# Blockwise attention, then hash-routed experts, on one core: transposes a pair earlier, and another order of weight loads

## The chip, the core and the metric

The kernel runs on one core of a Trainium2 chip. A core has a matrix engine (TensorE), three engines for elementwise work (VectorE, ScalarE, GpSimd), an engine that mainly issues transfers (SyncE), and 16 DMA engines that all of them share. Each engine takes its own instructions in order; they wait for each other by semaphores. On-chip memory is SBUF (operands) and PSUM (where TensorE writes its results).

The metric is the device time of one execution in microseconds (us). Before the change it is 337.07 us, the median of three runs (336.7 to 337.87).

## What is computed

Attention over 8 batches of 8 heads, 576 positions, head width 64, masked by blocks of 64; then every one of the 4608 rows of width 512 goes through one of 8 experts, chosen by a hash of its token id.

```python
scores = scale * np.matmul(q, k.transpose(0, 1, 3, 2))
mask = block_i >= block_j
attn = np.exp(scores - max)           # masked, then divided by the row's sum
x = (attn @ v) as rows [B * S, H * D]
expert_idx = token_ids * 2654435761 % 8
for e in range(8):
    xe = x[expert_idx == e]
    out[expert_idx == e] = np.maximum(xe @ w1[e], 0.0) @ w2[e]
```

## The kernel before

The order of all instructions is written out by hand; each engine runs its own share of that one list.

**Attention.** The work is cut into 32 pairs of heads, `g` from 0 to 31, four pairs to a batch; the loop at L505 has one turn for each and one more to drain. In turn `g` TensorE makes the scores of pair `g` in three chunks (`S_chunk`, L191), ScalarE takes the exponential of each chunk (L200), and TensorE multiplies the exponentials of pair `g - 1` by the values (`PV`, L227). The values carry a column of ones, so that the row sums come out of the same matmul. VectorE divides (`norm`, L247: a reciprocal at L254, a product at L255). `S_rest` (L202) makes the last diagonal block of all four pairs of a batch at once.

The scores need q and k with the head width on the partitions. `T_group(b, n)` (L150) makes a quarter of that for batch `b`: 18 transposes on TensorE (L159), then one copy out of PSUM on VectorE (L164; for batch 0 half of it on ScalarE). Groups 2 and 3 are k, 0 and 1 are q. The four groups of batch `b` stand at the ends of turns `4b - 4` to `4b - 1`, that is, up to the last turn before the batch begins. There is one PSUM buffer (`tp`) for them and one (`O`) for the outputs; score chunks have two.

**Loads.** `load_qk` and `load_v` fetch a batch on GpSimd's queue and turn it into bf16 on the way: two transfers of 576 KB for k and q, six for v. Each transfer from that queue takes the next of eight semaphores in turn, and waits until the transfer that had it before has landed. A finished batch of rows is written to a DRAM buffer by `write_x` (L260), the first five batches from SyncE, the last three from GpSimd.

**Routing.** `route()` (a generator, advanced step by step in the first turns) works out the place of each token in a table of 640 places per expert. Then for each batch `j` `place_a` (VectorE, turn `5 + 2j`), `place_p` (GpSimd, turn `6 + 2j`) and `place_b` (turn `9 + 2j`) add the rows to the table `perm3`. `place_b` is five matmuls (L412) into spare columns of the `O` buffer, and a sum into `acc` on VectorE (L415). It stands ahead of `PV`.

**Experts.** For each expert, rows are fetched by `perm3` (`gather_x`, L461, five indirect transfers of 128 rows), transposed (`transpose_x`, L553 and L554), multiplied by the first weights and passed through the relu (`stage_a`, L566 and L571; for experts 0 and 1 in two parts, L585 and L589), multiplied by the second weights (`stage_b`, L599), copied out of PSUM (L604) and scattered to the output (L606, five indirect transfers). The loop runs `stage_a(e)`, `transpose_x(e + 1)`, `stage_b(e - 1)`. There are two buffers for first weights and two for second ones, so `load_w1(e + 2)` waits for `stage_a(e)` to end, and the gathers for expert `e + 2` stand behind it on GpSimd, and the scatters of expert `e - 1` behind those.

The SBUF of the attention's buffers is used again for the experts' ones, so the first copy at L554 waits until the last rows are out of it.

Of the kernel before, what the change touches and what calls it, by code (L numbers as in the profile page):

```python
# [10 lines left out]
F32 = mybir.dt.float32  # L11
# [23 lines left out]
WARM = 40  # L35
# [5 lines left out]
def kernel(  # L41
# [30 lines left out]
    ov_i = const.tile([1, OVT + 1], I32, name="ov_i")  # L72
    inc = const.tile([P, E], F32, name="inc")

    nc.gpsimd.iota(jmp[:], pattern=[[1, P]], base=0, channel_multiplier=-1,
                   allow_small_or_imprecise_dtypes=True)
    nc.vector.tensor_single_scalar(identbf[:], jmp[:], 0.0, op=ALU.is_equal)
    nc.vector.tensor_single_scalar(lower[:], jmp[:], 0.0, op=ALU.is_gt)
    nc.vector.memset(onesbf[:], 1.0)

    nc.vector.memset(maskk[:], 0.0)
    nc.vector.memset(maskq[:], 0.0)
# [144 lines left out]
    def PV(g, m):  # L227
        b, pr = divmod(g, NP)
        h = pr + NP * m
        pt = pts[g % 2]  # L230
        vx, v4 = vexts[b % NV]
        if g not in ots:
            ots[g] = psO.tile([P, 2, 512], F32, name="O", tag="O")
        O = ots[g][:, m, 0 : 5 * (D + 1)].rearrange("p (t d) -> p t d", t=5)
        for t in range(5):
            for n, (o0, i) in enumerate(PVS[t]):
                nc.tensor.matmul(  # L237
                    O[:, t, :], lhsT=pt[:, m * PTW + o0 : m * PTW + o0 + 128], rhs=vx[:, h, i, 0 : D + 1],
                    start=(n == 0), stop=(n == t),
                )  # L240
            if t == 4:
                nc.tensor.matmul(
                    O[:, t, :], lhsT=pt4s[b % 2][:, pr * 64 : pr * 64 + 128],
                    rhs=v4[:, pr, m, 0 : D + 1], start=False, stop=True,
                )

    def norm(g):  # L247
        b, pr = divmod(g, NP)
        if b not in xss:
            xss[b] = xfix[b % 3]  # L250
        xs = xss[b]
        O = ots.pop(g)[:, :, 0 : 5 * (D + 1)].rearrange("p m (t d) -> p m t d", t=5)
        rs = att.tile([P, 2, 5, 1], F32, name="rs", tag="rs")
        nc.vector.reciprocal(rs[:], O[:, :, :, D : D + 1])  # L254
        nc.vector.tensor_tensor(  # L255
            out=xs[:].rearrange("p t (m r d) -> p r m t d", m=2, r=NP)[:, pr],
            in0=O[:, :, :, 0:D], in1=rs[:].to_broadcast([P, 2, 5, D]), op=ALU.mult,
        )
# [146 lines left out]

    def place_b(b, g):
        ohp, ohg, _ = places.pop(b)
        ots[g] = psO.tile([P, 2, 512], F32, name="O", tag="O")
        pq = ots[g][:, 0, 512 - 2 * NG :]
        for i in range(5):  # L410
            n = P if i < NT else 64
            nc.tensor.matmul(pq, lhsT=ohp[0:n, i, :],  # L412
                             rhs=ohg[0:n, i, :, :].rearrange("p w g -> p (w g)"),
                             start=(i == 0), stop=(i == 4))
        nc.vector.tensor_tensor(out=acc[:].rearrange("p w g -> p (w g)"),  # L415
                                in0=acc[:].rearrange("p w g -> p (w g)"), in1=pq, op=ALU.add)

# [27 lines left out]
    w1s, w2s = {}, {}  # L445

    def load_w1(e):
        w1b = wts.tile([P, DM // P, FF], BF16, name="w1b", tag="w1b")
        nc.gpsimd.dma_start(w1b[:], moe_w1[e].rearrange("(p db) f -> p db f", p=P))  # L449
        w1s[e] = w1b  # L450

# [5 lines left out]
    def gather_x(e, t0=0, t1=G):  # L457
        n = N if t1 > GA else BA * S
        for t in range(t0, t1):
            g = e * G + t  # L460
            nc.gpsimd.indirect_dma_start(  # L461
                out=xgs[g % (2 * G)][:], out_offset=None, in_=x_dram[0:n, :],
                in_offset=bass.IndirectOffsetOnAxis(ap=perm3[:, g : g + 1], axis=0),
                bounds_check=n - 1, oob_is_err=False,
            )


    NPAIRS = B * NP
    nc.sync.dma_start(tid[:], moe_token_ids.rearrange("(b s) -> b s", b=B))
    rgen = route()  # L470
    next(rgen)
    load_qk(0)
    load_v(0)
    load_qk(1)
    load_v(1)
    warm = psS.tile([P, 2, 512], F32, name="warm", tag="ps")
    for n in range(WARM):
        nc.tensor.matmul(warm[:, 0, 0:P], lhsT=onesbf[:], rhs=onesbf[:], start=True, stop=True)
    T_group(0, 2)
    T_group(0, 3, pool=(psO, "O"))  # L480
    T_group(0, 0, pool=(psS, "ps"))
    T_group(0, 1, pool=(psS, "ps"))

    Ts = {g: [] for g in range(NPAIRS + 1)}
    for b in range(1, B):
        for z, n in enumerate((2, 3, 0, 1)):
            Ts[4 * b - 4 + z].append((b, n))
    steps = {g: [] for g in range(NPAIRS + 1)}
    steps[0] += [lambda: next(rgen), lambda: next(rgen)]
    steps[1].append(lambda: next(rgen))  # L490
# [6 lines left out]
        mids[9 + 2 * j] = j  # L497
    steps[24].append(placed)
    loads = {g: [] for g in range(NPAIRS + 1)}
    for b, at in ((2, 0), (3, 4), (4, 7), (5, 10), (6, 13), (7, 16)):  # L500
        loads[at].append((load_qk, b))
        loads[at + 1].append((load_v, b))
    for g, what in ((19, (load_w1, 0)), (20, (load_w1, 1)), (24, (load_w2, 0)), (27, (load_w2, 1))):
        loads[g].append(what)
    for g in range(NPAIRS + 1):  # L505
        b, pr = divmod(g, NP)
        live = g < NPAIRS
        if live:
            S_chunk(g, 0)
            S_chunk(g, 1)  # L510
        if g in mids:
            place_b(mids[g], g - 1)
        if g >= 1:
            PV(g - 1, 0)
            PV(g - 1, 1)
            norm(g - 1)
        if live:
            S_chunk(g, 2)
            if pr == 0:
                S_rest(b)  # L520
        for bn in Ts[g]:
            T_group(*bn)
        for step in steps[g]:
            step()
        if pr == 0 and b >= 1:
            write_x(b - 1)
        if 12 <= g < 12 + 2 * G:
            nc.gpsimd.memset(xgs[g - 12][:], 0.0)
        if g in (26, 27):
            gather_x(g - 26, 0, GA)  # L530
        for load, n in loads[g]:
            load(n)
    att_ctx.close()
# [94 lines left out]
    load_w1(3)  # L628
    stage_b(0)
    load_w2(2)  # L630
    transpose_x(2)
    for e in range(2, E):
        stage_a(e)
        if e + 2 < E:
            load_w1(e + 2)
        if e + 1 < E:
            transpose_x(e + 1)
        if e + 2 < E:
            gather_x(e + 2)
        stage_b(e - 1)  # L640
        if e + 1 < E:
            load_w2(e + 1)
        if e == 3:
            over()
    stage_b(E - 1)
# [2 lines left out]
    n_ov = nc.values_load(ov_i[0:1, 0:1], min_val=0, max_val=OVT)  # L648
    with tc.For_i(0, n_ov, 1) as j:
        eo = nc.values_load(ov_i[0:1, bass.ds(j + 1, 1)], engines=[ET.Pool], min_val=0, max_val=E - 1)  # L650
        w1b = wts.tile([P, NKT, FF], BF16, name="w1b", tag="w1b")
        nc.gpsimd.dma_start(
            w1b[:], moe_w1[bass.ds(eo, 1)].rearrange("e (p db) f -> p (e db) f", p=P))
        w2b = wts.tile([P, NFT, DM], BF16, name="w2b", tag="w2b")
        nc.gpsimd.dma_start(
            w2b[:], moe_w2[bass.ds(eo, 1)].rearrange("e (p fb) o -> p (e fb) o", p=P))
        idx = mx.tile([P, 1], I32, name="idx", tag="idx", bufs=1)
        nc.vector.tensor_copy(idx[:], perm3[:, bass.ds(j + E * G, 1)])
        xg = xgs[0]
        nc.gpsimd.indirect_dma_start(  # L660
            out=xg[:], out_offset=None, in_=x_dram[:, :],
            in_offset=bass.IndirectOffsetOnAxis(ap=idx[:, 0:1], axis=0),
            bounds_check=N - 1, oob_is_err=False,
        )
        xt = mx.tile([P, NKT, P], BF16, name="xt", tag="xt", bufs=1)
        tp = psY.tile([P, NKT, P], BF16, name="tp", tag="yp")
        for db in range(NKT):
            nc.tensor.transpose(out=tp[:, db, :], in_=xg[:, db::NKT], identity=identbf[:])
        nc.vector.tensor_copy(xt[:], tp[:])
        ht = mx.tile([P, NFT, P], BF16, name="ht", tag="ht", bufs=1)  # L670
        for ft in range(NFT):
            hp = psY.tile([P, P], F32, name="hpo", tag="yp")
            for db in range(NKT):
                nc.tensor.matmul(hp[:], lhsT=w1b[:, db, ft::NFT], rhs=xt[:, db, :],
                                 start=(db == 0), stop=(db == NKT - 1))
            nc.scalar.activation(ht[:, ft, :], hp[:], ACT.Relu)
        yp = psY.tile([P, DM], F32, name="ypo", tag="yp")
        for ft in range(NFT):
            nc.tensor.matmul(yp[:], lhsT=ht[:, ft, :], rhs=w2b[:, ft, :],
                             start=(ft == 0), stop=(ft == NFT - 1))  # L680
        ysb = mo.tile([P, DM], F32, name="ysb", tag="ysb")
        nc.vector.tensor_copy(ysb[:], yp[:])
        nc.gpsimd.indirect_dma_start(
            out=out[:, :], out_offset=bass.IndirectOffsetOnAxis(ap=idx[:, 0:1], axis=0),
            in_=ysb[:], in_offset=None, bounds_check=N - 1, oob_is_err=False,
        )
# [30 lines left out]
```

The softmax here doesn't subtract the row's maximum and nothing guards it: scores larger than these inputs give would overflow.

## Time and profile before

| | |
|---|---|
| time, median of 3 (lowest, highest) | 337.07 us (336.7, 337.87) |
| span of the profiled execution | 337.6 us |
| first scores of pair 0; of pair 4 | 14.82 us; 34.88 us |
| first scores of pair 24 | 113.08 us |
| last product (L255) of the attention ends | 149.05 us |
| first copy of gathered rows (L554) | 153.18 us |
| last scatter issued | 327.70 us |
| busy: TensorE, VectorE, ScalarE, GpSimd | 78%, 41%, 42%, 50% of the span |

How to read the lines further down. In the slices each of 40 digits is the busy share of 8.44 us in tenths. A line of the timeline has the start, the busy time, the engine, the line of the kernel, the operation, output and input with their shapes, and a count; the bracket gives the idle time before it and what ended that. A line of the waits has the waiting engine and line, the one it waited for, the sum in us, the number of times, and the longest. A line of the windows has the stretch, its length, the busy time and number of instructions of TensorE's matmuls, its weight loads, VectorE, ScalarE and GpSimd, then TensorE's granted clock, the DMA's share and GB/s. The DMA's share can be over 1, since several packets of one engine are under way at a time.

### The profile page before, as it was taken

Reading aid. Unit: us, or ns where it says so; the run is one execution under the profiler, and the core shown is the slowest. Engines: PE = TensorE matmul, PEld = TensorE weight load, DVE = VectorE, ACT = ScalarE, POOL = GpSimd, SP = SyncE. Lnnn points to the kernel's source line nnn. Section 1 sums busy time; section 2 is a strip of 40 time slices with the busy share of each in tenths; the row PEclk is TensorE's granted clock in tenths of the full one; section 3 lists DMA queues with packets and bytes.
Section 4 is the critical chain, followed back from the end, with each engine's and each line's share of the span. In section 5 each row is a group of like instructions: output and inputs, shape, how many; then the busy total and the mean of one; then the engine's idle time right before and its main releaser. Section 6 shows DMA issues by size and latency. Waiting matters only on the chain. (4 is left out here: it accounts for less than half of the span.)

```text
span 337.6 us, 7650 instructions
## 1 busy us (share of the span) xinstructions
PE 263.3 (78%) x3255; PEld 195.2 (58%) x3255; DVE 138.5 (41%) x263; ACT 143.3 (42%) x173; POOL 167.9 (50%) x217
## 2 busy tenths in 40 slices
PE   1749768786878765747789899799798897999970
PEld 1637656575756654535576594675666746668430
DVE  6347696777777544321111414033132140330430
ACT  1437768686868655832252060330320503314000
POOL 8838937949950252116237507437257174050550
PEclk9958999999999995896799999999799999999996
DMA  7999699999999098212109979677766786337330
GB/s 104 181 185 171 109 196 227 136 207 186 190 190 228 34 213 165 80 62 59 47 19 209 188 191 221 176 141 220 160 108 229 139 217 179 66 140 127 128 132 12
DMA packets 53571, 50.36 MB, mean 149 GB/s; under 512 B 40098, under 2 KB 44004, under 8 KB 51488
## 3 DMA queue, kind: packets, MB, share of 16 engines
q0 software_dynamic: 50480, 46.87, 78.2%
q1 hardware_dynamic: 3056, 2.99, 2.9%
q8 instruction: 26, 0.43, 0.5%
q14 instruction: 9, 0.07, 0.1%
HBM read 67.15 MB, written 15.20 MB: 244 GB/s over the span
## 5 line engine op out<-in xcount | busy, mean ns | idle before, releaser
L200 ACT ACTIVATE pt<-ps 128x1024 bf16<-128x1024 f32 x96 | 92.6, 1026 | 36.8 <-PE ps L182 33.0
L571 ACT ACTIVATE hT<-hp 128x640 bf16<-128x640 f32 x48 | 33.3, 703 | 95.3 <-PE hp L566 82.5
L599 PE MATMUL yp<-w2b,hT 128*128 128x512 bf16 x320 | 70.2, 379 | 0.0
L566 PE MATMUL hp<-xT,w1b 128*128 128x320 bf16 x384 | 56.2, 304 | 9.0 <-ACT hT L571 6.7
L566 PEld LDWEIGHTS <-w1b 128*128 128x128 bf16 x384 | 52.6, 145 | 12.6 <-issue 10.4
L606 POOL DMA_INDIRECT out_dram<-ysb,perm x40 | 39.8, 994 | 38.8 <-DVE ysb L604 32.2
L461 POOL DMA_INDIRECT xg<-x_dram,perm x40 | 40.5, 1013 | 26.7 <-issue 14.1
L172 PE MATMUL ps<-qT,kT 64*128 64x512 bf16 (+4 forms) x320 | 37.2, 307 | 20.5 <-DVE qT L164 10.2
L599 PEld LDWEIGHTS <-hT 128*128 128x128 bf16 x320 | 31.1, 98 | 36.1
L604 DVE COPY ysb<-yp 128x512 f32<-128x512 f32 x40 | 27.7, 692 | 55.9 <-PE yp L599 47.7
L554 DVE COPY xT<-tpx 128x512 bf16<-128x512 bf16 x40 | 15.5, 420 | 74.2 <-PE tpx L553 68.3
L237 PE MATMUL O<-vx,pt 128*128 128x65 bf16 x896 | 36.1, 197 | 7.8 <-DVE acc L415 3.9
L237 PEld LDWEIGHTS <-pt 128*128 128x128 bf16 x896 | 32.4, 100 | 10.2 <-issue 7.1
L172 PEld LDWEIGHTS <-kT 64*128 64x128 bf16 x320 | 13.3, 95 | 31.3 <-DVE qT L164 12.9
L124 POOL DMA_DIRECT2D vx<-in_v_dram x32 | 28.6, 914 | 0.3 <-issue 0.2
L255 DVE TENSOR_TENSOR xs<-O,rs 128x640 bf16<-128x640 f32 x32 | 26.4, 824 | 1.1
L164 DVE COPY kT<-tp 128x1152 bf16<-128x1152 bf16 (+1 forms) x16 | 20.4, 1283 | 13.5 <-PE tp L159 13.5
L585 PE MATMUL hp<-xT,w1b 128*128 128x384 bf16 (+1 forms) x128 | 21.1, 329 | 3.2 <-DVE xT L554 3.2
L449 POOL DMA_DIRECT2D w1b<-in_moe_w_dram x8 | 4.7, 589 | 35.3 <-PE tpx L553 35.3
L164 DVE COPY qT<-tp 128x1152 bf16<-128x1152 bf16 (+1 forms) x16 | 20.4, 1280 | 3.3 <-PE ps L182 2.6
L589 ACT ACTIVATE hT<-hp 128x768 bf16<-128x768 f32 (+1 forms) x16 | 11.3, 704 | 23.4 <-PE hp L585 11.0
L553 PE MATMUL tpx<-identbf,xg 128*128 128x128 bf16 x160 | 13.7, 220 | 9.1 <-DVE xT L554 7.8
(107 smaller groups left out, 241.3 us busy)
## 6 DMA issues: line engine op xcount, KB each, us to landing
w1b<-in_moe_w_dram POOLq DMA_DIRECT2D x8, 1024.0 KB
w2b<-in_moe_w_dram POOLq DMA_DIRECT2D x8, 1024.0 KB
vx<-in_v_dram POOLq DMA_DIRECT2D x32, 128.0 KB
kb<-in_k_dram POOLq DMA_DIRECT2D x7, 576.0 KB
qb<-in_q_dram POOLq DMA_DIRECT2D x7, 576.0 KB
x_dram<-xs SPq DMA_DIRECT2D x5, 512.0 KB, 8.1
x_dram<-xs POOLq DMA_DIRECT2D x3, 512.0 KB
xg<-x_dram,perm POOLq DMA_INDIRECT x40
```

The lines of the kernel that those rows point to most:

```text
L124: nc.gpsimd.dma_start(vx[:, :, i, 0:D], v[b, :, 128 * i : 128 * i + 128, :].rearrange("h p d -> p h d"))
L164: copy(qkTs[b][w][:].rearrange("p r (j c) -> p (r j) c", c=RUN)[:, r0:r1, c0 : c0 + n], tp[:, 0:n, r0:r1].rearrange("p c r -> p r c"))
L172: nc.tensor.matmul(ps[:, m, o0 : o0 + n], lhsT=kT[rows, pr, 128 * kt : 128 * kt + 128], rhs=qT[rows, pr, q0 : q0 + n], start=first, stop=F ...
L200: nc.scalar.activation(ptv[:, :, 512 * ch : 512 * ch + 512], ps[:], ACT.Exp, scale=SCALE)
L237: nc.tensor.matmul(O[:, t, :], lhsT=pt[:, m * PTW + o0 : m * PTW + o0 + 128], rhs=vx[:, h, i, 0 : D + 1], start=(n == 0), stop=(n == t),)
L255: nc.vector.tensor_tensor(out=xs[:].rearrange("p t (m r d) -> p r m t d", m=2, r=NP)[:, pr], in0=O[:, :, :, 0:D], in1=rs[:].to_broadcast([ ...
L461: nc.gpsimd.indirect_dma_start(out=xgs[g % (2 * G)][:], out_offset=None, in_=x_dram[0:n, :], in_offset=bass.IndirectOffsetOnAxis(ap=perm3[ ...
L566: nc.tensor.matmul(hp[:, t, 0:HC], lhsT=w1b[:, db, ft::NFT], rhs=xT[:, db, t * HC : (t + 1) * HC], start=(db == 0), stop=(db == NKT - 1),)
L571: nc.scalar.activation(hT[:, ft, :].rearrange("p (t n) -> p t n", t=2), hp[:, :, 0:HC], ACT.Relu)
L599: nc.tensor.matmul(yp[:], lhsT=hT[:, ft, tt * P : (tt + 1) * P], rhs=w2b[:, ft, :], start=(ft == 0), stop=(ft == NFT - 1),)
L604: nc.vector.tensor_copy(ysb[:], yp[:])
L606: ins = nc.gpsimd.indirect_dma_start(out=out[:, :], out_offset=bass.IndirectOffsetOnAxis(ap=perm3[:, gg : gg + 1], axis=0), in_=ysb[:], in ...
```

## The change

It has five parts.

- The warm-up matmuls, and the ones tile that they read, come first, ahead of the routing's first step.
- Transpose groups end a pair earlier: those of batch `b` stand in turns `4b - 5` to `4b - 2`. For batches 1 and 2, whose data comes late, there is a list of its own, with a new place (`z = 0`) between the score chunks and the outputs. Batch 2's loads move back accordingly.
- The sum of the row table follows the outputs: `place_b` comes after `PV`, and its sum, now `place_c`, after `norm`.
- First weights have three buffers. `load_w1(e + 3)` follows `load_w2(e + 1)` at the end of the loop's turn, so the gathers no longer stand behind a load that waits for `stage_a(e)`.
- The first experts' loads and gathers move: second weights of expert 0 from turn 24 to 22, of expert 1 from 27 to 29, first weights of expert 1 from 20 to 21, the two early gathers from turns 26 and 27 to 28 and 29.

```diff
+    nc.vector.memset(onesbf[:], 1.0)
     nc.gpsimd.iota(jmp[:], pattern=[[1, P]], base=0, channel_multiplier=-1,
...
-    nc.vector.memset(onesbf[:], 1.0)
...
     def place_b(b, g):
         ohp, ohg, _ = places.pop(b)
-        ots[g] = psO.tile([P, 2, 512], F32, name="O", tag="O")
...
+        return pq
+
+    def place_c(pq):
         nc.vector.tensor_tensor(out=acc[:].rearrange("p w g -> p (w g)"),
...
-        w1b = wts.tile([P, DM // P, FF], BF16, name="w1b", tag="w1b")
+        w1b = wts.tile([P, DM // P, FF], BF16, name="w1b", tag="w1b", bufs=3)
...
+    warm = psS.tile([P, 2, 512], F32, name="warm", tag="ps")
+    for n in range(WARM):
+        nc.tensor.matmul(warm[:, 0, 0:P], lhsT=onesbf[:], rhs=onesbf[:], start=True, stop=True)
     rgen = route()
...
-    Ts = {g: [] for g in range(NPAIRS + 1)}
+    Ts = {(g, z): [] for g in range(NPAIRS + 1) for z in range(2)}
     for b in range(1, B):
-        for z, n in enumerate((2, 3, 0, 1)):
-            Ts[4 * b - 4 + z].append((b, n))
+        at = {1: ((1, 1), (2, 0), (2, 1), (3, 0)), 2: ((4, 1), (5, 1), (6, 0), (6, 1))}.get(
+            b, tuple((4 * b - 5 + z, 1) for z in range(4)))
+        for n, gz in zip((2, 3, 0, 1), at):
+            Ts[gz].append((b, n))
...
-    for b, at in ((2, 0), (3, 4), (4, 7), (5, 10), (6, 13), (7, 16)):
-        loads[at].append((load_qk, b))
-        loads[at + 1].append((load_v, b))
-    for g, what in ((19, (load_w1, 0)), (20, (load_w1, 1)), (24, (load_w2, 0)), (27, (load_w2, 1))):
+    for b, g in enumerate((1, 4, 7, 10, 13, 16), 2):
+        loads[g].append((load_qk, b))
+        loads[g + 1 if b > 2 else 3].append((load_v, b))
+    for g, what in ((19, (load_w1, 0)), (21, (load_w1, 1)), (22, (load_w2, 0)), (29, (load_w2, 1))):
...
-        if g in mids:
-            place_b(mids[g], g - 1)
+        for bn in Ts[g, 0]:
+            T_group(*bn)
         if g >= 1:
             PV(g - 1, 0)
             PV(g - 1, 1)
+            if g in mids:
+                pq = place_b(mids[g], g - 1)
             norm(g - 1)
+            if g in mids:
+                place_c(pq)
...
-        for bn in Ts[g]:
+        for bn in Ts[g, 1]:
             T_group(*bn)
...
-        if g in (26, 27):
-            gather_x(g - 26, 0, GA)
+        if g in (28, 29):
+            gather_x(g - 28, 0, GA)
...
     load_w2(2)
+    load_w1(4)
     transpose_x(2)
     for e in range(2, E):
         stage_a(e)
-        if e + 2 < E:
-            load_w1(e + 2)
         if e + 1 < E:
             transpose_x(e + 1)
...
         if e + 1 < E:
             load_w2(e + 1)
+        if e + 3 < E:
+            load_w1(e + 3)
```

More of the change, by code (lines that the diff above doesn't have):

```diff
@@ L475 @@
     load_v(1)
-    warm = psS.tile([P, 2, 512], F32, name="warm", tag="ps")
-    for n in range(WARM):
-        nc.tensor.matmul(warm[:, 0, 0:P], lhsT=onesbf[:], rhs=onesbf[:], start=True, stop=True)
     T_group(0, 2)
@@ L650 @@
         eo = nc.values_load(ov_i[0:1, bass.ds(j + 1, 1)], engines=[ET.Pool], min_val=0, max_val=E - 1)
-        w1b = wts.tile([P, NKT, FF], BF16, name="w1b", tag="w1b")
+        w1b = wts.tile([P, NKT, FF], BF16, name="w1b", tag="w1b", bufs=3)
         nc.gpsimd.dma_start(
```

## The prediction

> **What bounds the kernel now.** I read the page's slices first (part 2), then the summed waits, then the timeline of one batch, then two-microsecond windows of the DMA, then ScalarE's timeline in the expert stages. The chain that ended last holds only the final loop, so it is of no use here.
>
> The slices show two regimes. Attention runs to about slice 17 (149 us) and no engine is full in it. The DMA is, from slice 1 to 12, and then idle in slice 13.
>
> ```profile
> PE   1749768786878765747789899799798897999970
> ...
> DVE  6347696777777544321111414033132140330430
> ACT  1437768686868655832252060330320503314000
> ...
> DMA  7999699999999098212109979677766786337330
> ```
>
> The summed waits name the attention gaps: TensorE waits for a transposed-query copy (L164) 7 times for 1.46 us, and for the row-table sum (L415) 8 times for 0.5 us.
>
> ```profile
> PE ps L172 <- DVE qT L164: 10.2, 7, 1.5
> ...
> PE O L237 <- DVE acc L415: 3.9, 8, 0.6
> ...
> PEld L318 <- DVE cnt L316: 3.3, 1, 3.3
> ...
> PE tp L159 <- DMA kb<-in_k_dram: 0.9, 1, 0.9
> ```
>
> The timeline at pairs 15 and 16 shows both. The sum at 77.77 stands behind a copy on VectorE, and pair 15's outputs stand behind the sum. The last query copy starts at 80.23, and pair 16's first scores wait for it until 81.64.
>
> ```profile
> 76.50 1.35 DVE L164 COPY qT<-tp 128x1152 bf16<-128x1152 bf16 x1
> ...
> 77.77 0.29 DVE L415 TENSOR_TENSOR acc<-acc,O 128x144 f32<-128x144 f32 x1
> ...
> 78.11 0.58 PE L237 MATMUL O<-vx,pt 128*128 128x65 bf16 x14 [0.58 <-DVE acc L415]
> ...
> 80.23 1.36 DVE L164 COPY qT<-tp 128x1152 bf16<-128x1152 bf16 x1
> ...
> 81.64 0.39 PE L172 MATMUL ps<-qT,kT 64*128 64x512 bf16 x2 [1.46 <-DVE qT L164]
> ```
>
> The windows (last three columns: clock, DMA share, GB/s) show 73 us of near-continuous DMA at 192 GB/s, then a hole.
>
> ```profile
> 3.00:34.00 31.00, 19.61 (x361) 16.25 (x361) 17.20 (x53) 14.39 (x17) 22.78 (x36) 0.83 1.57 173
> 36.70:110.00 73.30, 57.82 (x1319) 46.18 (x1316) 57.16 (x87) 57.02 (x63) 47.77 (x67) 1.00 1.37 192
> 110.00:116.20 6.20, 4.30 (x117) 3.58 (x115) 3.38 (x5) 3.67 (x5) 0.02 (x1) 1.00 0.01 3
> ```
>
> In the expert stages ScalarE takes a first-layer tile every 1.08 us for expert 7 (301.92, 302.94, 304.03), but for expert 5 the second comes 2.78 us after the first:
>
> ```profile
> 259.24 0.70 ACT L571 ACTIVATE hT<-hp 128x640 bf16<-128x640 f32 x1 [11.85 <-PE hp L566]
> 262.02 1.30 ACT L571 ACTIVATE hT<-hp 128x640 bf16<-128x640 f32 x2 [2.07 <-PE hp L566]
> ```
>
> One more line decides where the expert part begins: the first copy of gathered rows waits for the last attention rows to be in DRAM.
>
> ```profile
> 153.18 0.76 DVE L554 COPY xT<-tpx 128x512 bf16<-128x512 bf16 x2 [4.12 <-DMA x_dram<-xs]
> ```
>
> **What the Trainium skill says.** "Perfetto Trace Analysis", Optimization Strategy: the same gap repeating on an engine that should be saturated can mean that buffers are short. The repeated 1.46 us agrees in form, but here it is order, not buffers: the copy is issued in the last pair before use. "DMA: Bandwidth & Descriptors", Issuing engines are not separate DMA queues: all transfers share the same 16 engines whoever issues them. The trace agrees: SyncE's row writes fall inside stretches in which GpSimd's loads run, and 192 GB/s is for both. "TensorE: Matmul & The Clock Gate", What's actually happening: after an idle window the clock falls to half. The trace agrees: a clock of 0.50 at 18 to 26 us and 130 to 136 us, each time after a gap.
>
> **Start.** The 40 warm-up matmuls (4.0 us) run at 7.26 to 11.26, and the first transposes wait behind them. Moved ahead of `route()`, they need only the ones tile and end near 5.5 us. What remains is the transfer: GpSimd's issue for batch 1's q waited until 11.54 for batch 0's second q half, so that half landed near 11.5. The last transposes then take 0.6 us (1.2 at half clock) and the two half copies 0.75 each: first scores near 13.3, not 14.82. Batch 1's keys land at 18.45, seen the same way. Before, TensorE waits for them inside pair 0, VectorE's routing sums queue behind their copy, and the routing matmul L318 waits for those, so pair 1 begins at 22.85. Now pair 0 has no transposes, and pair 1 begins near 16.8. Its pairs run at about 3.6 us (part of them at half clock), so pair 4 begins near 27.5, not 34.88: 7.4 us gained, give or take 2.
>
> **Steady pairs.** Four pairs took 15.8 us (97.46 minus 81.64). VectorE's steps, start to start: reciprocal 0.25, product 0.75, copy 1.3, and in odd pairs 1.2 for `place_a` and 0.3 for the sum: 2.3 + 3.8 = 6.1 us in two pairs, 12.2 in a batch. ScalarE needs 12 x 0.94 + 0.4 = 11.7, TensorE about 11.6. With transposes a pair ahead, the boundary wait (1.46) goes; with the sum after the outputs, its two waits per batch (2 x 0.5) go. That leaves 13.3, near the floor of 12.2, and I take 13.0. The new place of the sum costs nothing: the next outputs need that bank only some 1.6 us later, behind S_chunk 2, a transpose group and two score chunks. Five batches (pairs 4 to 23): 65 us, not 78.2. Pairs 24 to 31: 8 x 3.0 = 24 (ScalarE's pace), then 2.3 for the last outputs. Attention computes until 27.5 + 65 + 24 + 2.3 = 119, against 149.05.
>
> **The DMA then binds.** Loads for batches 3 to 7, two first weights and five row writes moved in 36.7 to 110. Now they start when batch 2's values land, near 33.5, and the queue stays full: to 33.5 + 73.3 - 1.5 (a slack at 60 to 64 us) = 105.3. The second-layer weights of expert 0, moved to pair 22, follow: 1 MB at 210 GB/s (226 to 230 us show 209 to 213) = 5 us, 110.3. Batch 5's rows: 2.2 us at 265 GB/s plus about 0.8 to be seen: 113.3. Six gathers issue at 1.3 us each: 121.1. Expert 1's second weights, 0.6 + 5: 126.7. Batch 7's rows stand behind them on the same queue: 2.2 + 0.8, so the first L554 copy comes near 130, and not at 119 + 4 = 123. Against 153.18 that is 23 us less.
>
> **Expert part.** It took 337.6 - 153.18 = 184.4 us. Expert 7's first layer is the norm: first activation 1.35 us after the first matmul, last one 7.54 later. Experts 3, 4, 5 and 6 lose 2.4, 4.4, 2.4 and 2.4 against it: 11.5 us. In those four, and not in 2 and 7, GpSimd's issues have run back to back for 11 us (weights, five gathers at 1.3, five scatters at 1.3) and are still running. The third buffer frees the gathers and first weights from the end of the stage: they go out right after the scatters of the expert before, which then come one by one as for expert 7. I expect the pattern of experts 2 and 7 everywhere: 184.4 - 11.5 = 173. The cause of the stall isn't shown by any wait, so the saving lies between 0 and 11.5; I take all. The DMA allows it: an expert moves 4.1 MB, some 17 us of DMA at measured rates in a period of 19.3. Loading two weights back to back costs nothing: the first is used a stage later, the second three.
>
> **Sum.** 130 + 173 = 303 us.
>
> **Rivals.** (B) The stall stays, because scatters and weights still fall in the first layer: 130 + 184.4 = 314. For: its cause is unnamed. Against: experts 2 and 7 issue the same kinds without it. (C) Attention is starved: the eight transfers of a batch let GpSimd issue only when those of the batch before have landed, row-table products queue behind it, and key transposes stop TensorE for a few us in each batch; expert part from 140, stall half gone: 140 + 178 = 318. (D) The row write isn't held by the weights: 124 + 173 = 297. (E) Slower: keys land only just in time for the old order. Asked for one pair (3.95 us) sooner in six batches, they cost 23.7, against 10.2 + 3.9 + 3 gained; nothing from the stall: 337 + 6.6 = 344. Against: only 0.9 us of such waits, all at the start; by the sums above batch 7's keys land near 87 and are asked for near 90. The margin is thin.
>
> **Numbers.** A 0.45, B 0.25, C 0.15, D 0.10, E 0.05. The range: 294 (D and a little more) to 321 (C and a little more) leaves out E and the tails. Faster 0.94, same 0.01, slower 0.05.
>
> **What would show it.** Right: no L172 wait on L164 at batch starts, none of L237 on L415, pair 4 near 27 us, batches of about 13 us with VectorE nearly full, DMA busy without the hole, an idle TensorE of some 10 us before L554's first copy near 130, and 1.08 us steps for every expert. Wrong: L159 waits on kb or qb in mid-attention, or steps of over 2 us in experts 3 to 6.

## The result and the profile after

The changed kernel takes 316.31 us (median, 315.69 to 317.08), the kernel before 337.47 beside it: ratio 0.936, 95% interval 0.930 to 0.942. Later runs gave the kernel before about 343 us and the changed one 316.78: ratio 0.921 (0.915 to 0.926). The experiments below ran in three groups, beside which the kernel before took 343.4, 343.0 and 342.9 us, so I read their times against that 316.78 (ratios are to the kernel before). A few runs were about 1% longer than the others of their kernel, the profiled ones of "two w1 buffers" and "all three" among them: the ratios leave such runs out, the medians don't, and from those two traces I read patterns, not totals.

The slices of the changed kernel, 7.85 us each, for the same four engines and the DMA, with the granted TensorE clock:

```profile
PE   5687699998989874629889899989999899999960
...
DVE  6657988997997831220111404123141240411430
ACT  1676859998989985404243060330603306033000
...
PEclk9769989999999999658799999999999999999996
DMA  6997999999999914823049995595895968155330
```

Counted from 0, VectorE shows 7 to 9 in slices 3 to 13, where it mostly had 6 and 7. Slices 15 and 16 are low on all three engines: that is the stop described below. Slice 17 is the wait for the last rows (a slice was 8.44 us before, so the same slice is some 10 us earlier now). The clock is low from slice 16 to 19 (and in slices 1, 2 and 5).

The summed waits: the wait for a query copy at batch starts is gone (the one of 0.9 us that is left is at the first scores of pair 0, at 12.77), and no wait of L237 for the row-table sum is listed any more. Two "remote" waits, for which the profile found no releasing instruction, are among the largest that remain in attention.

```profile
ACT pt L200 <- PE ps L182: 17.7, 27, 4.2
...
DVE rs L254 <- remote: 7.3, 1, 7.3
...
ACT pt L200 <- remote: 4.5, 1, 4.5
...
PE ps L172 <- DVE qT L164: 0.9, 1, 0.9
```

The timeline around the start of pair 16 (columns: start, duration, engine, line). The pair's first scores (72.02) follow without a wait, the row-table sum (72.22) stands behind the product of pair 14 (71.48), and the copies of the next batch's keys fill VectorE.

```profile
71.48 0.82 DVE L255 TENSOR_TENSOR xs<-O,rs 128x640 bf16<-128x640 f32 x1
72.02 0.39 PE L172 MATMUL ps<-qT,kT 64*128 64x512 bf16 x2
72.22 0.30 DVE L417 TENSOR_TENSOR acc<-acc,O 128x144 f32<-128x144 f32 x1
72.43 1.35 DVE L164 COPY kT<-tp 128x1152 bf16<-128x1152 bf16 x1
```

Two of the stretches of before and a third (columns: bounds, length, busy time of PE, PEld, DVE, ACT, GpSimd; clock, DMA share, GB/s):

```profile
36.70:110.00 73.30, 65.03 (x1484) 52.37 (x1481) 63.30 (x93) 62.27 (x69) 50.29 (x69) 0.98 1.45 205
110.00:116.20 6.20, 4.38 (x100) 3.54 (x100) 2.99 (x5) 5.38 (x7) 0.00 (x0) 1.00 0.17 63
122.00:127.00 5.00, 1.06 (x15) 0.56 (x13) 0.20 (x1) 0.47 (x2) 3.62 (x4) 1.00 0.35 98
```

In the first stretch VectorE works 63.3 of 73.3 us (57.2 before). The DMA moves 205 GB/s there and is again nearly idle from 110 to 116. The third stretch is the stop: TensorE works 1.06 of 5 us, at a granted clock of 1.00, and the DMA has a share of 0.35.

ScalarE in expert 5 has steps of 1.02 and 1.09 us where one was 2.78:

```profile
239.01 0.70 ACT L579 ACTIVATE hT<-hp 128x640 bf16<-128x640 f32 x1 [11.10 <-PE hp L574]
240.03 0.70 ACT L579 ACTIVATE hT<-hp 128x640 bf16<-128x640 f32 x1 [0.32 <-issue]
241.12 0.70 ACT L579 ACTIVATE hT<-hp 128x640 bf16<-128x640 f32 x1 [0.38 <-PE hp L574]
```

And the expert part begins 13.7 us sooner, again at the landing of the last row write, 4.5 us after the last attention product ends (134.95):

```profile
134.13 0.82 DVE L255 TENSOR_TENSOR xs<-O,rs 128x640 bf16<-128x640 f32 x1
...
139.49 0.76 DVE L562 COPY xT<-tpx 128x512 bf16<-128x512 bf16 x2 [4.53 <-DMA x_dram<-xs]
```

Set beside the forecast's milestones, in the profiled run (span 314.1 us; its time was 315.69):

| step | before | forecast | measured |
|---|---|---|---|
| first scores of pair 4 | 34.89 | 27.5 | 28.90 |
| pairs 4 to 7 | 14.96 | 13.0 | 17.00 |
| pairs 8 to 23 | 63.23 | 52.0 | 53.81 |
| pairs 24 to 27 | 19.76 | 12.0 | 12.60 |
| pair 28 to the last product's end | 16.2 | 14.3 | 22.6 |
| from there to the first L562 copy (L554 before) | 4.1 | 11.2 | 4.5 |
| from that copy to the end | 184.4 | 173 | 174.6 |

Pair starts are the first score matmuls of the pair (L172, 64x512); differences of two of them give the rows. Two rows are much longer than forecast. Their lines follow.

Pairs 4 to 7, the timeline at pair 6. The first three VectorE lines shown are the first and the last of the routing tail's six operations and the product of pair 4; the key copy, whose transposes were done at 35.75, starts at 37.50, and the next transposes wait for it until 38.90, with pair 5's outputs behind them. ScalarE has nothing to do for 4.21 us:

```profile
34.11 0.76 DVE L361 TENSOR_REDUCE slf<-cum 128x40 f32<-128x320 f32 x1
...
36.23 0.47 DVE L369 CAST slo<-sj 128x40 bf16<-128x40 int32 x1
...
36.76 0.82 DVE L255 TENSOR_TENSOR xs<-O,rs 128x640 bf16<-128x640 f32 x1
...
37.50 1.35 DVE L164 COPY kT<-tp 128x1152 bf16<-128x1152 bf16 x1
...
38.90 1.17 PE L159 MATMUL tp<-identbf,qb 128*64 128x128 bf16 x18 [2.02 <-DVE kT L164]
...
42.45 2.00 ACT L200 ACTIVATE pt<-ps 128x1024 bf16<-128x1024 f32 x2 [4.21 <-PE ps L182]
```

Part of the 4.21 us is the clock. It was 0.50 from 38.7 to 42.1 us: the 18 transposes took 1.17 us, where they take 0.69 at full clock. In three later profiles with the same order in these pairs and a clock of 1.00 there (the experiments "only expert 1's second weights", "rows in memory of their own" and "gathers paced") ScalarE's gap is 2.85 to 2.88 us, and pairs 4 to 7 take 15.7 us, not 17.0.

Pair 28 to the end. The last output matmul of pair 29 starts at 121.89; VectorE's reciprocal, which needs nothing else, starts at 126.80. Score matmuls of the next chunks are recorded up to 123.16, and ScalarE takes the first of them at 126.95. In between GpSimd issues gathers and one weight transfer:

```profile
118.18 1.10 POOL L463 DMA_INDIRECT xg<-x_dram,perm  x1 [0.35 <-issue]
...
121.89 0.19 PE L242 MATMUL O<-v,pt 128*128 128x65 bf16 x1
...
124.82 1.00 POOL L463 DMA_INDIRECT xg<-x_dram,perm  x1 [0.30 <-issue]
125.83 0.62 POOL L456 DMA_DIRECT2D w2b<-in_moe_w_dram  x1
126.80 0.22 DVE L254 RECIPROCAL rs<-O 128x10 f32<-128x10 f32 x1 [7.30 <-remote]
126.95 2.86 ACT L200 ACTIVATE pt<-ps 128x1024 bf16<-128x1024 f32 x3 [4.53 <-remote]
...
128.02 0.61 PE L172 MATMUL ps<-qT,kT 64*128 64x448 bf16 x4 [4.67 <-ACT pt L200]
```

The kernel before had such a stop at its early gathers, in two parts, with the granted clock at 0.50 afterwards: the first scores of pairs 27 and 28 were 10.5 us apart (122.31 and 132.84).

```profile
120.73 1.10 POOL L461 DMA_INDIRECT xg<-x_dram,perm  x1 [2.65 <-issue]
...
124.29 1.02 ACT L200 ACTIVATE pt<-ps 128x1024 bf16<-128x1024 f32 x1 [2.58 <-PE ps L182]
...
127.36 1.00 POOL L461 DMA_INDIRECT xg<-x_dram,perm  x1 [0.31 <-issue]
...
127.96 1.02 ACT L200 ACTIVATE pt<-ps 128x1024 bf16<-128x1024 f32 x1 [2.64 <-remote]
```

### The profile page after: what moved, and what is told of

It reads as the page before. It is cut to its first block, busy times and chain, and to the rows that moved or that the text cites. A ratio compares the mean times of both kernels' runs of the same rounds, so it can differ in the third digit from the quotient of the medians.

```text
span 314.1 us, 7645 instructions
## 1 busy us (share of the span) xinstructions
PE 262.8 (84%) x3255; PEld 197.2 (63%) x3255; DVE 139.7 (44%) x263; ACT 144.4 (46%) x173; POOL 168.9 (54%) x217
## 3 DMA queue, kind: packets, MB, share of 16 engines
q0 software_dynamic: 50480, 46.87, 82.2%
## 5 line engine op out<-in xcount | busy, mean ns | idle before, releaser
L574 PE MATMUL hp<-xT,w1b 128*128 128x320 bf16 x384 | 53.3, 299 | 0.4 <-DVE xT L562 0.4
L172 PE MATMUL ps<-qT,kT 64*128 64x512 bf16 (+4 forms) x320 | 38.5, 306 | 16.1 <-ACT pt L200 14.7
L562 DVE COPY xT<-tpx 128x512 bf16<-128x512 bf16 x40 | 15.5, 421 | 66.2 <-PE tpx L561 60.3
L237 PE MATMUL O<-vx,pt 128*128 128x65 bf16 x896 | 37.5, 200 | 2.1 <-issue 1.3
L237 PEld LDWEIGHTS <-pt 128*128 128x128 bf16 x896 | 33.0, 102 | 4.7 <-issue 1.8
L172 PEld LDWEIGHTS <-kT 64*128 64x128 bf16 x320 | 14.5, 95 | 26.4 <-issue 18.4
L164 DVE COPY kT<-tp 128x1152 bf16<-128x1152 bf16 (+1 forms) x16 | 20.5, 1281 | 2.9 <-PE tp L159 2.9
L182 PE MATMUL ps<-maskq,maskk 64*128 64x64 bf16 x256 | 21.3, 193 | 0.3 <-issue 0.3
L164 DVE COPY qT<-tp 128x1152 bf16<-128x1152 bf16 (+1 forms) x16 | 20.5, 1281 | 1.8 <-PE tp L159 1.6
```

Of the source, the lines that this page charges most:

```text
L164: copy(qkTs[b][w][:].rearrange("p r (j c) -> p (r j) c", c=RUN)[:, r0:r1, c0 : c0 + n], tp[:, 0:n, r0:r1].rearrange("p c r -> p r c"))
L172: nc.tensor.matmul(ps[:, m, o0 : o0 + n], lhsT=kT[rows, pr, 128 * kt : 128 * kt + 128], rhs=qT[rows, pr, q0 : q0 + n], start=first, stop=F ...
L237: nc.tensor.matmul(O[:, t, :], lhsT=pt[:, m * PTW + o0 : m * PTW + o0 + 128], rhs=vx[:, h, i, 0 : D + 1], start=(n == 0), stop=(n == t),)
L574: nc.tensor.matmul(hp[:, t, 0:HC], lhsT=w1b[:, db, ft::NFT], rhs=xT[:, db, t * HC : (t + 1) * HC], start=(db == 0), stop=(db == NKT - 1),)
```

## The experiments

The theory after the first reading had four parts. The parts of the change gain separately and about what the prediction gave each. The crowded VectorE queue costs pairs 4 to 7 some 3 us. The stop in the last pairs belongs to the gathers. And the wait for the last rows comes from reused memory. The rivals stand with each run. Each edit is shown against the changed kernel.

**Two w1 buffers.** Each expert's w1 is issued after the first layer again.

```diff
-        w1b = wts.tile(..., tag="w1b", bufs=3)
+        w1b = wts.tile(..., tag="w1b")
...
     for e in range(2, E):
         stage_a(e)
+        if e + 2 < E:
+            load_w1(e + 2)
...
-        if e + 3 < E:
-            load_w1(e + 3)
```

> The changed kernel with two first-layer weight buffers again, each expert's w1 issued right after the first layer of the expert two before, as in the kernel before; attention stays changed. Theory (the stalls of experts 3 to 6 come with those back-to-back issues, 9.5 to 11.5 us): the expert part goes from 174.9 back to about 184.4 us, 326 us in all, with second activations over 2 us after the first in experts 3 to 6. Rival (the buffers are worth nothing, the expert part shrank for another reason): 316 us, plus or minus 1.5.

Measured: 326.65 us (ratio 0.951, 0.946 to 0.957), 9.9 us over the changed kernel. Expert 4's first activations, from ScalarE's lines in the timeline, are 2.80 us apart again, as in the kernel before:

```profile
223.22 0.70 ACT L579 ACTIVATE hT<-hp 128x640 bf16<-128x640 f32 x1 [12.38 <-PE hp L574]
...
226.02 1.30 ACT L579 ACTIVATE hT<-hp 128x640 bf16<-128x640 f32 x2 [2.09 <-PE hp L574]
```

The third buffer with its order removes the stall. Buffer and order were not separated.

**Transposes in the old pairs.**

```diff
-        at = {1: ((1, 1), (2, 0), (2, 1), (3, 0)), 2: ((4, 1), (5, 1), (6, 0), (6, 1))}.get(
-            b, tuple((4 * b - 5 + z, 1) for z in range(4)))
+        at = tuple((4 * b - 4 + z, 1) for z in range(4))
```

> The changed kernel with each batch's four transpose groups again in the four pairs just before their use (key group 0 of batch b in pair 4b-4), sums and all else as changed. Theory (the 1.46 us wait at each batch start is order, and pair 0 pays for batch 1's keys): about 1.5 us in each of 7 batches, some 10 us in all: 326 us, with waits of L172 for the query copy back at the batch starts. Rival (VectorE's total work sets the pace and the order is worth nothing; the two groups that pair 6 now holds even cost): 314 to 318 us.

Measured: 326.46 us (0.954, 0.948 to 0.961), 9.7 us over. In its summed waits the wait at the batch starts is back (eight times with that of pair 0):

```profile
PE ps L172 <- DVE qT L164: 12.2, 8, 1.8
```

Pair 4 starts at 34.02 (5.1 us later), pairs 4 to 7 take 15.1 us (1.9 less, the stall of pair 6 is gone), and pairs 8 to 23 take 58.4, 4.6 more: 1.15 us for each of four batches. So half of what this part gains lies in the first four pairs.

**The sum ahead of the outputs.**

```diff
+        ots[g] = psO.tile([P, 2, 512], F32, name="O", tag="O")
...
+        if g in mids:
+            place_c(place_b(mids[g], g - 1))
         if g >= 1:
             PV(g - 1, 0)
             PV(g - 1, 1)
-            if g in mids:
-                pq = place_b(mids[g], g - 1)
             norm(g - 1)
-            if g in mids:
-                place_c(pq)
```

> The changed kernel with the row-table matmuls and their sum ahead of the pair's output matmuls again. Theory of the prediction: two waits of 0.5 us in each batch come back, over four batches of table work: 320 us, with L237 waiting for the sum. Rival (with VectorE nearly full, the outputs would wait for the pair before's product in the same bank anyway): 316 to 317 us, plus or minus 1.

Measured: 320.54 us (0.934, 0.928 to 0.939), 3.8 us over. Pairs 8 to 23 take 57.7 us, 3.8 more, and the listed waits have the size that the kernel before showed:

```profile
PE O L237 <- DVE acc L418: 3.6, 8, 0.6
```

The 4.6 and 3.8 us of the last two experiments set one profile beside another, and pairs 8 to 23 vary: ten other profiled runs with the changed kernel's order there took 54.1 to 56.8 us. Against the longest of them 1.6 and 0.8 us are left. That the waits come back is shown by the lines; what they cost a batch is known only roughly.

**Warm-up late.** The 40 warm-up matmuls stand behind `route()`'s first part and the loads of the first two batches again.

```diff
-    warm = psS.tile([P, 2, 512], F32, name="warm", tag="ps")
-    for n in range(WARM):
-        nc.tensor.matmul(warm[:, 0, 0:P], ...)
     rgen = route()
...
     load_v(1)
+    warm = psS.tile([P, 2, 512], F32, name="warm", tag="ps")
+    for n in range(WARM):
+        nc.tensor.matmul(warm[:, 0, 0:P], ...)
     T_group(0, 2)
```

> The changed kernel with the 40 warm-up matmuls issued after the first routing steps again (they ran at 7.3 to 11.3 us there). Theory: first scores 1.5 to 2 us later (15.3, not 13.3), but pair 1 waits for batch 1's keys no longer, and some of the delay comes back in the crowded pairs 4 to 6: 316.5 to 318.5 us. Rival (the start's whole gain of 6.4 us up to pair 4 is the warm-up's): 321 to 323 us.

Measured: 319.21 us (0.926, 0.919 to 0.933), 2.4 us over, with overlapping intervals. First scores come at 14.79, not 12.77; by the product of pair 7 (49.65) 0.4 to 0.9 us of that are left against the two profiles of the changed kernel (49.23 and 48.78). The rival's 5 us are out; how much of the 2.4 is real these runs don't tell.

The four undone parts lose 9.9 + 9.7 + 3.8 + 2.4 = 25.8 us; the whole change gains 342.93 - 316.78 = 26.2 in the group of that 316.78. By the ratios it is 28 against 27. They add up, but each of the four is known to some 2 us or more, so what the loads and gathers that moved with them are worth isn't measured.

**Gathers one in a pair**, and expert 1's second weights in pair 23.

```diff
-    ... (22, (load_w2, 0)), (29, (load_w2, 1))):
+    ... (22, (load_w2, 0)), (23, (load_w2, 1))):
...
-        if g in (28, 29):
-            gather_x(g - 28, 0, GA)
+        if 25 <= g < 25 + 2 * GA:
+            e, t = divmod(g - 25, GA)
+            gather_x(e, t, t + 1)
```

> The changed kernel with the six early gathers issued one in each of pairs 25 to 30 instead of three in pairs 28 and three in 29, and expert 1's second-layer weights fetched in pair 23. Theory 1 (the stop of TensorE, ScalarE and VectorE at 122 to 127 us comes with a burst of issues on GpSimd): the stop goes, and with it part of the slow clock after it: 308 to 311 us. Theory 2 (every gather costs the others about 0.7 us wherever it stands): 315 to 317 us, with six small stops.

Measured: 314.72 us (0.920, 0.913 to 0.927), 2.1 us less, with overlapping intervals. The edit didn't do what its name says. Batch 5's row write was issued at 102.41, behind the weights of two experts, and the first gather, which needs those rows, went out only at 119.81; the DMA moved over 200 GB/s from 103 to 112 us, and single packets were still under way after 118. Six gathers then went out as three, the row write of batch 6, and three. In place of one stop ScalarE has two, the second at half clock:

```profile
119.81 1.10 POOL L463 DMA_INDIRECT xg<-x_dram,perm  x1 [16.08 <-DVE xs L255]
...
124.32 2.86 ACT L200 ACTIVATE pt<-ps 128x1024 bf16<-128x1024 f32 x3 [2.40 <-remote]
...
129.67 1.02 ACT L200 ACTIVATE pt<-ps 128x1024 bf16<-128x1024 f32 x1 [2.49 <-PE ps L182]
```

Neither theory was tested as meant.

**Only expert 1's second weights earlier** (the first edit of the experiment above alone).

> The changed kernel with only expert 1's second-layer weights moved, from behind the gathers in pair 29 to pair 23; the gathers stay where they are. Theory 1 (the stop comes with the burst of gathers): it stays, shorter by at most the 0.6 us of that issue: 315.5 to 316.5 us. Theory 3 (the stop comes with the megabyte of weights that follows the gathers): the stop goes: 308 to 311 us.

Measured: 315.95 us (0.924, 0.920 to 0.929), 0.8 less. The stop stays, and without any weight transfer behind the gathers:

```profile
119.99 1.10 POOL L463 DMA_INDIRECT xg<-x_dram,perm  x1 [1.53 <-DMA x_dram<-xs]
...
125.80 0.22 DVE L254 RECIPROCAL rs<-O 128x10 f32<-128x10 f32 x1 [5.67 <-remote]
...
126.63 1.00 POOL L463 DMA_INDIRECT xg<-x_dram,perm  x1 [0.30 <-issue]
128.75 2.86 ACT L200 ACTIVATE pt<-ps 128x1024 bf16<-128x1024 f32 x3 [6.25 <-remote]
```

So the weights are not its cause. VectorE came free while a gather was still to be issued, ScalarE only after the last.

**Batch 2's groups a pair earlier.**

```diff
-        at = {..., 2: ((4, 1), (5, 1), (6, 0), (6, 1))}.get(
+        at = {..., 2: ((3, 1), (4, 1), (5, 1), (6, 1))}.get(
```

> The changed kernel with batch 2's transpose groups in pairs 3, 4, 5 and 6 (one each) instead of 4, 5, 6 and 6. Theory (ScalarE's gap of 4.2 us that ends at 42.45 is VectorE's queue: the routing tail of 2.6 us stands ahead of a key copy, and the second group of pair 6 waits for that copy): 2 to 4 us gained, 312.5 to 314.5 us. Rival (VectorE's work in pairs 4 to 7 is the same in any order): 316 us, plus or minus 0.7.

Measured: 314.64 us (0.921, 0.914 to 0.928), 2.1 us less by the times, with overlapping intervals. In the profile pair 7's reciprocal starts at 45.27, in the other three of this group at 46.87 to 47.50 (in the first profile, with its stretch at half clock, at 48.53). The routing tail is about as long (2.4 us), but no transposes wait for the copy behind it, and ScalarE's gap is 0.95 us:

```profile
35.58 0.47 DVE L369 CAST slo<-sj 128x40 bf16<-128x40 int32 x1
...
36.85 1.35 DVE L164 COPY qT<-tp 128x1152 bf16<-128x1152 bf16 x1
...
38.37 0.69 PE L159 MATMUL tp<-identbf,qb 128*64 128x128 bf16 x18
38.54 2.91 ACT L200 ACTIVATE pt<-ps 128x1024 bf16<-128x1024 f32 x3 [0.95 <-PE ps L182]
```

Pairs 4 to 7 take 13.8 us here, and 14.0 and 14.8 in the two combinations below that have the same edit; without it they take 15.7 to 17.1 in all profiled runs that are otherwise alike there. So the order is worth some 2 us; of the 3.3 us by which ScalarE's gap shrank against the first profile, 1.4 are the clock's (4.21 to 2.85).

**Rows in memory of their own.**

```diff
-        xfix.append(fix.tile([P, 5, DM], BF16, name=f"xs{z}"))
+        xfix.append(const.tile([P, 5, DM], BF16, name=f"xs{z}"))
```

> The changed kernel with the three tiles of attention rows (xs) in memory of their own, which the expert part doesn't reuse. Theory (the first copy of gathered rows at 139.5 us waits for the last row write only because the memory of xs is reused): it comes about 4 us sooner, at 135.5, and the gathers that need the last rows hide behind the first layers of experts 0 and 1: 312 to 313 us. Rival (the late gathers or another release hold it all the same): 316 us, plus or minus 0.7.

Measured: 314.23 us (0.916, 0.909 to 0.922), 2.6 us less; intervals overlap at the edge. The first copy of gathered rows starts 1.65 us after the last product starts, not 5.36 (139.49 - 134.13), and waits for its transposes, no longer for a row write. Of these 3.7 us the time shows 2.6; the expert part behind them takes 175.5 us, not 174.6:

```profile
135.12 0.82 DVE L255 TENSOR_TENSOR xs<-O,rs 128x640 bf16<-128x640 f32 x1
...
136.77 0.80 DVE L562 COPY xT<-tpx 128x512 bf16<-128x512 bf16 x2 [0.83 <-PE tpx L561]
```

**The changed kernel again, and three combinations.** The first of them joins the last two edits.

> The changed kernel as it is, beside the others of this call: 316 to 319 us, whatever the theory; the three others are read against it.

> The changed kernel with both edits that each seemed to gain: batch 2's transpose groups in pairs 3, 4, 5, 6, and the attention rows in memory of their own. Theory (they act in different stages, 3.3 us in pairs 4 to 7 and 3.7 us between the last product and the first copy of gathered rows): 7 us less than the unchanged one, 309 to 311 us. Rival (what is gained early is lost again in the last pairs, because the gathers wait for the DMA): 3 us less.

Measured: 316.78 us (0.921, 0.915 to 0.926) and 311.54 us (0.907, 0.903 to 0.912). The 5.2 us gained lie between the theory's 7 and the rival's 3; the intervals don't touch, so the gain is real.

**Gathers paced.**

```diff
-        eng = nc.sync if b < BA - 1 else nc.gpsimd
+        eng = nc.sync if b < BA else nc.gpsimd
...
-    ... (22, (load_w2, 0)), (29, (load_w2, 1))):
+    ... (22, (load_w2, 0)), (23, (load_w2, 1))):
...
-        if g in (28, 29):
-            gather_x(g - 28, 0, GA)
+        if 26 <= g < 26 + 2 * GA:
+            nc.gpsimd.tensor_copy(tick[:], xss[(g - 1) // NP][:, 0, (g - 1) % NP * D : (g - 1) % NP * D + 1])
+            e, t = divmod(g - 26, GA)
+            gather_x(e, t, t + 1)
```

> The changed kernel with the six early gathers one in each of pairs 26 to 31, each behind a one-element GpSimd copy that waits for that pair's rows, so that they can't pile up; batch 5's row write goes to SyncE's queue so that it doesn't land behind four megabytes of weights, and expert 1's second-layer weights are fetched in pair 23. Theory 1 (it is back-to-back issues that stop the others): no stop of TensorE, ScalarE and VectorE over 1.5 us in pairs 26 to 31, the last product 5 to 7 us sooner than in the unchanged one, 310 to 312 us. Theory 2 (each gather costs the others 0.7 us or more): a small stop in each of the six pairs, no gain over 1.5 us.

Measured: 312.16 us (0.910, 0.906 to 0.915), 4.6 us less. The intervals just don't touch. Again the first gather came late (118.82), although the row write was now on SyncE's queue: it took 13.1 us from issue (104.39) to landing. The section of the Trainium skill that the prediction used ("DMA: Bandwidth & Descriptors", Issuing engines are not separate DMA queues) would have said so: the weights of another queue fill the same 16 engines, and this run agrees. Two gathers and a row write went out together, then two gathers, and the last two alone. ScalarE's waits:

```profile
121.79 2.85 ACT L201 ACTIVATE pt<-ps 128x1024 bf16<-128x1024 f32 x3 [1.48 <-PE ps L183]
...
126.25 2.86 ACT L201 ACTIVATE pt<-ps 128x1024 bf16<-128x1024 f32 x3 [1.60 <-PE ps L183]
...
128.03 1.03 POOL L464 DMA_INDIRECT xg<-x_dram,perm  x1 [0.54 <-issue]
130.50 1.02 ACT L201 ACTIVATE pt<-ps 128x1024 bf16<-128x1024 f32 x1 [1.39 <-PE ps L183]
```

The first pair of gathers cost ScalarE 1.48 us. From 122.2 us on the clock was 0.50, and most of the 1.60 us before 126.25 is the clock's: the score matmuls that ScalarE needs were recorded up to 125.94. The lone gathers at 128.03 and 131.72 cost nothing that can be seen: the 1.39 us before 130.50 is what the changed kernel shows at half clock in the same place (1.40 before 131.20) with no gather near. The last product comes 2.7 us sooner (133.42 against 136.14 in the run beside it), not the 5 to 7 of theory 1. So the slow clock came without the long stop too.

**All three.**

> All three together: batch 2's groups a pair earlier, rows in their own memory, gathers paced. If the gains add up as theory 1 has it: 303 to 306 us. If the pacing is worth nothing: the same as without it, 309 to 311 us.

Measured: 305.94 us (0.890, 0.885 to 0.894), 10.8 us less than the changed kernel and 37 less than the one before. The gains of the two parts, 5.2 and 4.6, add up. This is the fastest version of the study. In its profiled run the gathers bunched more than in the one before, so the time speaks for the sum and not for a pacing that worked.

**What the runs say of the stop.** In order of gathers issued back to back: six, ScalarE stopped 4.53 us (changed kernel), 6.25 (second weights moved) and 3.9 to 4.7 in seven more profiled runs; three, 2.40 (one in a pair) and 2.90 (all three); two, 1.48 (paced) and 1.77 (all three); one, nothing. (The 2.49 and 1.60 us at half clock above are left out, since half clock alone makes some 1.4 of each.) In the kernel before and in "warm-up late" the six had two stops of 1.7 to 3.3 us instead of one. The stop grows with the number in a row, as theory 1 has it, and since the lone ones cost nothing, a fixed price for each gather is out. Instruction fetches don't fill it either: from 122 to 127 us the DMA of the changed kernel moved only packets that GpSimd had issued. But seven gathers in a row at 139.5 to 148.4 us of the changed kernel left ScalarE's last two steps there at 1.30 us each (VectorE's next copy, at 149.46, did come 0.9 us after its transposes). So the gathers are part of the cause and not all of it, and by what way they hold back the work of other engines no run shows.

## Why the prediction was right in direction and 13 us short

Direction and most of the mechanism were right, and the time lies within the range, between the times of rivals B and C but by neither's way: the stall is gone, and no transposes waited for keys in mid-attention. The milestones account for the difference: 303 + 16.1 (attention's end) - 6.7 (wait for the rows) + 1.6 (expert part) = 314.0, the span of 314.1; the time is 1.6 us more than the span.

- **Start: right, 1.4 us short.** First scores at 12.77 (13.3 forecast), pair 1 at 16.25 (16.8), pair 4 at 28.90 (27.5). Warm-up and transposes were rightly taken together, but most of the gain is the transposes': putting them back costs 5.1 us at pair 4, the warm-up less than 2.
- **Steady pairs: right.** (The outputs at 78.11 in the forecast's lines are pair 14's, made in turn 15, not pair 15's; the wait is the same.) 53.81 us for 16 pairs, 13.45 a batch against 13.0. The other profiled runs with this order took 13.5 to 14.2 a batch. The two terms were 1.46 for the boundary and 1.0 for the sums; undone, they cost 1.15 and 0.96 against this profile, and 0.4 and 0.2 against the longest of the others.
- **Batch 1 at 13.0: a mis-sized term.** I used the steady pace for five batches, but pairs 4 to 7 have the routing tail on VectorE (2.6 us from 34.11 to 36.70) and five transpose groups, two of them in pair 6. They took 17.0 us, and the kernel before 14.96. Of the 4.0 us over the forecast about 1.3 are the clock at 0.50 in pair 6 (15.7 us in profiles without it), and batch 2's groups moved one pair give about 2 back.
- **Pairs 24 to 31 at 3.0: the failed step.** "8 x 3.0 = 24 (ScalarE's pace)" and the last outputs at 2.3 gave 26.3 us; they took 35.2. Pairs 24 to 27 held the pace (12.60). The other 8.3 us are in the stretch of the stop after pair 29's outputs and of the slow clock that followed. With the gathers less bunched (three runs) that stretch took 20.5 to 20.7 us instead of 22.6, still with a slow clock; what the rest needs no run shows. The kernel before showed the same stop at its gathers (pairs 24 to 27 took 19.76 us there, ScalarE stopped 2.58 and 2.64 us, the clock was 0.50 after), and I named the slow clock without asking what had stopped TensorE. The change moves the gathers by two pairs, and the stop went with them.
- **"The DMA then binds": did not happen.** With attention ending at 134.95 and not at 119 the DMA was done long before: 0.17 of its share was used from 110 to 116 us. The first copy came 4.5 us after the last product's end, the bare row write that I had reckoned as "119 + 4". Whether the DMA would bind if attention ended at 119 isn't tested, but the late gathers of two experiments show that rows written behind the weights of two experts (4 MB) were gathered only 14 to 17 us after the write's issue (104.39 to 118.82, 102.41 to 119.81).
- **Expert part: right.** 174.6 us against 173, and the undone buffer gives 9.9 us for the 11.5 of the stall.

So rival C had the begin of the expert part (140, measured 139.5) by luck, since its starved attention didn't occur, and the likeliest case had its length.

## What to carry to other kernels

When a stage is forecast at its steady pace, list what is in it that the steady stage doesn't have (here a routing tail and six gathers), and look in the profile of before for what it cost there: a stop that moves with an operation is not removed by moving it. Memory that the next stage reuses is a wait without a data need; a tile of its own took 3.7 us off a boundary, and 2.6 off the time. Transfers that gate nothing soon (weights) delay the small ones that do (rows) when they are issued first, whichever queue the small ones are on.

## What the runs showed of the hardware that I had not expected

The kernel before took 337.5 us in the first comparison and 343 in the three later ones, while the changed kernel took 316.3 and 316.8: the gain was 21 us in one group of runs and 26 in the others. The three later groups ran on three different chips and agree within 0.5 us for the kernel before; the chip of the first comparison isn't on record, so the cause stays open. And VectorE took outputs up to 4.9 us after their last matmul was recorded (121.89 to 126.80) while GpSimd issued indirect gathers, with neither the DMA (share 0.35) nor the clock (1.00) at a limit.
